# Wider TensorE products in the first stage of a transformer layer kernel: one matmul of 64x128 for four of 64x32

## The chip, the cores and the metric

The kernel runs on one core of one Trainium2 chip. Its time is device microseconds of one execution; the time of a version is the median of several runs. A core has TensorE (in profiles PE for matmuls, PEld for loading the stationary operand), VectorE (DVE), ScalarE (ACT), GpSimd (POOL) and SyncE (SP), which here issues transfers. Matmuls write to PSUM banks; the others read them from there.

## The reference

A parallel transformer layer for 2048 rows of width 512: attention with 32 heads of 16, and an MLP with a hidden width of 1792, both from the same normalised input, summed with the input.

```python
xn = _layernorm(x, axis=-1)
return x + _A_ref(xn, A_wqkv, A_wo) + _B_ref(xn, B_w1, B_b1, B_w2, B_b2)

# _A_ref
qkv = (x @ wqkv).reshape(B, S, 3, H, Dh).transpose(2, 0, 3, 1, 4)
q, k, v = qkv[0], qkv[1], qkv[2]
scores = jnp.einsum("bhqd,bhkd->bhqk", q, k) * (Dh ** -0.5)
o = jnp.einsum("bhqk,bhkd->bhqd", _softmax(scores, axis=-1), v)
return o.transpose(0, 2, 1, 3).reshape(B, S, D) @ wo

# _B_ref
h = _gelu(jnp.einsum("bsd,df->bsf", x, w1) + b1)
return jnp.einsum("bsf,fd->bsd", h, w2) + b2
```

## The kernel before, in words

Numbers are held as two half-precision parts, so that a product of two matrices is three products of parts. Heads are worked on in 8 groups of four; the queries of a group in 4 blocks of 512. A group and a block are one of 32 *blocks* `t`. For each block the scores are computed twice: first as queries by keys, to find each query's maximum (`s_mm`, `s_max`), then as keys by queries (`e_half`), with the maximum already subtracted by extra rows of the operands, followed by the exponential on ScalarE (line 444) and the product with V (`v_half`). A *unit* `u` is a sixteenth of a block: 128 queries by 512 keys for four heads in the first use, 128 keys by 512 queries in the second. The second use runs 19 units (`LEAD`) behind the first.

**Array shape.** Operands of a head lie on 62 or 64 of the 128 rows, two heads above each other. `tiled` (line 200) makes a product of 64 rows from four matmuls of 64 rows by 32 columns, one for each quarter of the output partitions. A product for the upper half of the rows and one for the lower half go to different PSUM banks.

**First stage.** It loads and normalises x, transposes it, projects the first queries, keys and values, sums the absolute values of the weights on ScalarE to find their scales (`total`, line 937; each piece of weights is fetched by a transfer that ScalarE issues, three buffers `wch`), and computes the first 19 units of scores. Its instructions are added to a `Plan` with costs and dependencies; `plan.run` fixes the order on every engine from those costs before the program is built. Within it:
- `twelve` (line 1049) projects with full matmuls of 128x128;
- `side_by_side` runs two groups at once, one on the upper, one on the lower half of the rows, three products of each per step, with `tiled`; there are seven such pairs of groups (`PAIRED`), each of 2 groups x 12 products x 2 halves;
- `score` (line 1114) calls `s_mm` for two heads per step, four heads per unit, and VectorE takes the maximum of each result (line 403).

When the 16 units of block 0 are done, their maxima are reduced (line 369), split into two parts on GpSimd (371 to 373), transposed on TensorE by two small matmuls 32 columns wide (`m_turn`, line 377), copied (line 382), stored to memory (`m_store`, line 358) and read back as rows into the query operand (`m_rows`, line 363). The second use of block 0 needs them.

**Main loop.** From then on `unit` writes out the order by hand: score products, second score products, V products and products of a filler (remaining projections, then the MLP, then the output projection) in turn. All of them but a few at the very end go through 64x32 matmuls, which are recorded at line 174 (`product`), as those of the first stage are. At the very end one group (line 584) has products of 64 rows by 128 columns on one half of the rows.

In the block's query order before, a unit's 128 queries are two runs of 64: columns 64 x qt and 256 + 64 x qt of the block's 512. The layout of the maxima in memory (`m_d`) follows it.

Of the kernel before, what the change touches and what calls it, by code (L numbers as in the profile page):

```python
# [10 lines left out]
F16 = mybir.dt.float16  # L11
# [7 lines left out]
P = 128  # L19
# [8 lines left out]
QB = 512  # L28
NQB = S // QB
NG = H // 4  # L30
# [28 lines left out]
def layer_kernel(ctx: ExitStack, tc: tile.TileContext, x, wqkv, wo, w1, b1, w2, b2, out):  # L59
    nc = tc.nc  # L60
# [3 lines left out]
    def pool(stack, name, bufs=1, space=None, side=None):  # L64
        kw = {k: v for k, v in (("space", space), ("side", side)) if v is not None}
        return stack.enter_context(tc.tile_pool(name=name, bufs=bufs, **kw))
# [4 lines left out]
    dram = pool(ctx, "dram", space=DRAM)  # L71
# [4 lines left out]
    w1_d = dram.tile([NF // 2, P, 2, 2, NC, P], F16, name="w1_d")  # L76
    w2_d = dram.tile([P, 2, NF, D], F16, name="w2_d")
    acc_d = dram.tile([S, D], F32, name="acc_d")
    m_d = dram.tile([NG * NQB, 2, 2, 2, 8, P // 2], F16, name="m_d")
    ot_d = dram.tile([D, 2, S], F16, name="ot_d")  # L80
    den_d = dram.tile([NG * NQB, 2, 4, QB], F32, name="den_d")

# [5 lines left out]
    kst, qst = ([[const.tile([P, 2, QB], F16, name=f"{x}st{i}_{b}") for b in range(NQB)] for i in range(2)] for x in "kq")  # L88
# [83 lines left out]
    def product(user, *args, **kw):  # L172

        p = nc.tensor.matmul(*args, **kw)  # L174
        if user is None:
            return
        if user in goal:
            p._wait_ge(turns[user], counted[user])
            tc.declare_fence(p.ins, group=goal.pop(user))
        newest[user] = p  # L180
# [10 lines left out]
    def enter():  # L191

        for user, ps_ in left.items():
            if ps_:
# [2 lines left out]
                    tc.add_to_no_dep_group(goal[user], p.ins)  # L197
                ps_.clear()

    def tiled(user, dst, lhs, rhs, start, stop):  # L200

        for j in range(0, P, 32):
            product(user, dst[j:j + 32], lhs[:, j:j + 32], rhs, start=start, stop=stop)


    scale_of, wfs = {}, []
# [13 lines left out]
    class Plan:  # L220
# [7 lines left out]
        def add(self, engine, ns, fn, after=(), take=(), free=(), size=0, tail=0, gap=0, small=False, lag=0):  # L228
            t = dict(gap=gap, small=small, lag=lag, e=engine, ns=ns, fn=fn, after=[a for a in after if a], take=take, free=free, size=size, tail=tail,
                     end=None, n=len(self.todo))  # L230
            for key in free:
                self.users.setdefault(key, []).append(t)
            self.todo.append(t)
            return t
# [120 lines left out]
        slot[0] = now  # L355

    def m_store(t, turned):
        nc.sync.dma_start(m_d[t].rearrange("s a j r q -> (s a j r) q"), turned)

    def m_rows(t, a):  # L360
        g, qb = divmod(t, NQB)
        dst = qst[g % 2][qb][64 * a + 62:64 * a + 64].rearrange("j p (s n) -> j p s n", s=2)
        nc.sync.dma_start(dst, m_d[t, :, a].rearrange("s j (p t) q -> j p s (t q)", p=2))

    def m_parts(t):

# [13 lines left out]
    def m_copy(pt):  # L380
        turned = work.tile([64, 64], F16, name="mturned", bufs=2)
        nc.scalar.activation(turned, pt[:64, :64], AF.Copy)
        return turned

    def s_mm(u, n, s):

        t, i = divmod(u, 16)
        g, qb = divmod(t, NQB)
        qt, kb = divmod(i, 4) if t else (i % 4, i // 4)
        ks, qs = kst[g % 2], qst[g % 2]  # L390
        p, a = divmod(n, 2)
        r = slice(64 * a, 64 * a + 62)
        for j in range(0, P, 32):
            c = QB // 2 * (j // 64) + 64 * qt + j % 64
            product(None, s[j:j + 32], qs[qb][r, p, c:c + 32], ks[kb][r, p, :], start=True, stop=True)

    def s_max(u, n, s):

# [7 lines left out]
    def s_half(u, n):  # L406

        s = banks("S")
        s_mm(u, n, s)
        s_max(u, n, s)  # L410

    def s_end(u):

        t, i = divmod(u, 16)
        if i < 15:
            return
        steps, parts = m_parts(t)
        for step in steps:
            step()
        given("dve", 220)  # L420

        def store():

            fresh = cur[0] is not None and 0 < sum(cur[0].at) <= 4
            pt = banks("S" if fresh else "T")
            m_turn(pt, parts)
            m_store(t, m_copy(pt))
            for a in (1, 0):
                m_rows(t, a)

        stores[t] = store

    def e_half(u, n):

        p, a = divmod(n, 2)
        t, kt = divmod(u, 16)
        g, qb = divmod(t, NQB)
        st = banks("T")
        r = slice(64 * a, 64 * a + 64)
        k0 = (kt % 4) * P  # L440
        tiled(None, st, kst[g % 2][kt // 4][r, p, k0:k0 + P], qst[g % 2][qb][r, p, :], True, True)
        pe = work.tile([P, QB], F32, name="pe", bufs=12)
        ptiles[u, n] = pe
        nc.scalar.activation(pe, st, AF.Exp, scale=scale_of[g // 2])  # L444
        given("act", 520)
# [114 lines left out]
    class Group:  # L560
# [15 lines left out]
        def product(self, side):  # L576

            if self.bank is None:
                self.bank, self.key = self.alloc()
            lhs, rhs = self.prods[side % 2][self.at[side % 2]]()  # L580
            start = self.first and self.at == [0, 0]
            if side == 2:
                self.at = [min(self.at[0] + 1, n) for n in self.n]
                nc.tensor.matmul(self.bank, lhs, rhs, start=start, stop=self.last and self.over())
                return
            r = slice(64 * side, 64 * side + 64)
            self.at[side] += 1
            tiled("D", self.bank, lhs[r], rhs[r], start, self.last and self.over())
# [157 lines left out]
    class Halves:  # L746
# [6 lines left out]
        def product(self, side):  # L753
            k = self.at[side]
            if k == self.n[side]:
                return
            if self.banks[side] is None:
                self.keys.append(free_banks["S"].pop(0))
                self.banks[side] = bank_tile(self.keys[-1], "S")
            lhs, rhs = self.prods[side][k]()  # L760
            r = slice(64 * side, 64 * side + 64)
            self.at[side] += 1
            tiled(None, self.banks[side], lhs[r], rhs[r], k == 0, self.at[side] == self.n[side])
            if self.at == self.n:
                self.finish(*[b for b in self.banks if b is not None])
                free_banks["S"] += self.keys
# [84 lines left out]
    with ExitStack() as st1:  # L851
# [262 lines left out]
        def score(u):  # L1114

            t, i = divmod(u, 16)
            qt, kb = divmod(i, 4) if t else (i % 4, i // 4)
            for p in range(2):
                keys = [("S", u, 2 * p + a) for a in range(2)]

                def mm(keys=keys, u=u):
                    s_of[u] = True
                    for key in keys:
                        tl[key] = sb_tile(key)
                        s_mm(key[1], key[2], tl[key])

                old = m_prev[-4:-2]
                s_prev[0] = add("PE", 220, mm, [s_prev[0]] + k_ready[kb] + q_ready[t] + old, take=keys, gap=1230, small=True)
                for key in keys:
                    m_prev.append(add("DVE", 607, lambda key=key: s_max(key[1], key[2], tl[key]), [s_prev[0]], free=[key]))  # L1130
# [11 lines left out]
        for w in (1, 0):  # L1142
# [5 lines left out]
            else:  # L1148
                a = add("POOL", 800, lambda wf=wf, i1=i1: nc.gpsimd.tensor_scalar(tl[wf], tl[wf], i1, 0.0, op0=ALU.mult, op1=ALU.add), [h])
# [5 lines left out]
        a = add("DVE", 90, lambda: nc.vector.tensor_tensor(sexp[:, 0:1], fac0[:, 0:1], fac0[:, 1:2], op=ALU.mult), [chain])  # L1155
        a = add("DVE", 90, lambda: nc.vector.tensor_scalar_mul(sexp[:, 0:1], sexp[:, 0:1], DH ** -0.5), [a])
# [5 lines left out]
        a = add("DVE", 90, lambda: nc.vector.tensor_tensor(amv[:, 2:3], amv[:, 0:1], amv[:, 1:2], op=ALU.max), v_sum)  # L1162
# [54 lines left out]
        a = add("DVE", 220, m_steps[0], m_last)  # L1217
        for step in m_steps[1:]:
            a = add("POOL", 230, step, [a])
# [5 lines left out]
        a = add("PE", 100, turn_m, [a], take=[mkey], small=True)  # L1225
        a = add("ACT", 220, lambda: m_of.append(m_copy(tl[mkey])), [a], free=[mkey])
        put = add("SP", 480, lambda: m_store(0, m_of[0]), [a], size=4)
        for k in (1, 0):
            add("SP", 660, lambda k=k: m_rows(0, k), [put], size=4, tail=E_TAIL)
# [16 lines left out]
        for n, src in enumerate(every[:NM]):  # L1246
            key = ("wch", "m", n)
            dst = am_all[:, 12 + n:13 + n] if n < 2 else am_all[:, n - 2:n - 1] if n < 9 else amx[:, n - 2:n - 1]
# [5 lines left out]
                    nc.tensor.matmul(wp, wo_s[:, 0, 0, 0:P], wo_s[:, 0, 0, :], start=True, stop=True)  # L1254

        nc.vector.memset(wo_s[:, 0, 0, :], 0.0)
        plan.run(fill)
        wfs[1] = [tl["wq", 1, w] for w in range(2)]
        pos[0] = LEAD

# [330 lines left out]
```

## Time and profile before

| | us |
|---|---|
| median of 3 runs | 1458.61 |
| the runs | 1460.75, 1451.14, 1458.61 |
| the profiled execution's own time | 1454.41 |
| its span, first to last instruction | 1452.6 |
| PE busy in the span | 1431.1 (99%) |
| DVE busy | 1348.1 (93%) |
| ACT busy | 1256.6 (87%) |

The profile is of one execution. A row of the timeline has the start, the length, engine, line, operation, what is written and read, the shape (rows*columns of the stationary operand, then the moving operand), a count where several were merged, and in brackets the engine's idle time before it with what ended that. "issue" there means that the engine waited for nothing that the profile shows. PEclk is the share of full clock that TensorE was granted. Matmuls are pipelined: one lasts about 0.38 us from start to end, and the next can start before that.

### The profile page before, as it was taken

The numbers are of one execution on the slowest core, as the hardware profiler recorded it, in microseconds if no ns is written. First come the engines' busy times: TensorE is split into PE (matmuls) and PEld (weight loads), VectorE is DVE, ScalarE is ACT, GpSimd is POOL, SyncE is SP. The second block draws the span as 40 slices with busy tenths as digits, with TensorE's granted clock in tenths as the row PEclk, the third lists the DMA queues.
The fourth block names the chain that finished last, engine by engine and source line by source line (L and its number), as shares of the span: only waits on it lengthen the run. The fifth ranks groups of instructions, "written<-read, shape, count | busy, mean of one in ns | idle before, by whom it ended". The sixth has DMA issues, their size and how long they took to land.

```text
span 1452.6 us, 90738 instructions
## 1 busy us (share of the span) xinstructions
PE 1431.1 (99%) x41221; PEld 973.9 (67%) x41221; DVE 1348.1 (93%) x2236; ACT 1256.6 (87%) x2394; POOL 687.0 (47%) x774
## 2 busy tenths in 40 slices
PE   8889999999999999999999999999999999999998
PEld 4457777776667777666677766666666667666664
DVE  8769999999999999999999999999999999999933
ACT  6558888888999888899988899998889998888885
POOL 5101757664688411368841147783026787212210
PEclk9999999999999999999999999999999999999999
DMA  7550655555223111121122111122102210212313
GB/s 225 167 177 4 202 176 157 183 161 179 83 88 112 50 52 31 47 82 40 49 60 69 28 52 45 43 80 59 37 26 82 56 42 16 59 56 77 119 62 111
DMA packets 111482, 124.98 MB, mean 86 GB/s; under 512 B 21244, under 2 KB 83068, under 8 KB 111096
## 3 DMA queue, kind: packets, MB, share of 16 engines
q1 hardware_dynamic: 103896, 109.74, 24.8%
q10 hardware_dynamic: 7200, 9.44, 2.2%
q8 instruction: 322, 5.28, 1.5%
q14 instruction: 64, 0.52, 0.1%
HBM read 81.66 MB, written 37.34 MB: 82 GB/s over the span
## 4 chain that ended last, share of the span: by engine, by line
PE 92%; DVE 5%; ACT 1%; issue 1%; DMA 0%; SPq 0%; DVEq 0%; POOL 0%; ACTq 0%
PE pD L174 28%; PE pV L174 26%; PE pT L174 21%; PE pS L174 16%; DVE mt L403 4%; DMA wq<-in_A_wqkv_dram 0%; DVE xt L1032 0%; DVE bs L989 0%; ACT xs L1002 0%; PE pT L1049 0%; DVE wvh L1171 0%; ACT xt L1023 0%; ACT pe L444 0%; ACT pe L1002 0%; DVE ac L1466 0%
## 5 line engine op out<-in xcount | busy, mean ns | idle before, releaser
L403 DVE TENSOR_REDUCE mt<-pS 128x1 f32<-128x512 f32 x2029 | 1279.0, 682 | 42.3 <-PE pS L174 14.1
L444 ACT ACTIVATE pe<-pT 128x512 f32<-128x512 f32 x2048 | 1109.1, 599 | 140.1 <-PE pT L174 59.2
L174 PE MATMUL pV<-pe,vv 64*32 64x512 f32 x8192 | 1087.3, 591 | 0.3
L174 PE MATMUL pT<-qst,kst 64*32 64x512 f16 x8192 | 705.4, 378 | 0.6 <-ACT pe L444 0.3
L174 PE MATMUL pS<-kst,qst 62*32 62x512 f16 x8116 | 628.1, 378 | 1.3 <-issue 0.8
L174 PEld LDWEIGHTS <-qst 62*32 62x32 f16 x8192 | 312.4, 91 | 187.6 <-issue 37.9
L174 PE MATMUL pD<-xb,wc 64*32 64x512 f16 x5376 | 363.3, 376 | 0.0
L174 PE MATMUL pD<-w_s,g 64*32 64x512 f16 x5376 | 361.1, 376 | 0.0
L174 PEld LDWEIGHTS <-kst 64*32 64x32 f16 x8192 | 281.2, 91 | 97.0 <-issue 25.0
L174 PEld LDWEIGHTS pV<-pe,vv 64*32 64x32 f32 x8192 | 241.4, 106 | 12.6 <-PE pV L174 5.6
L174 PEld LDWEIGHTS <-wc 64*32 64x32 f16 x5376 | 160.7, 92 | 44.8 <-issue 0.3
L174 PEld LDWEIGHTS <-g 64*32 64x32 f16 x5376 | 162.9, 92 | 38.7
L174 PE MATMUL pD<-xt,wqk_h 64*32 64x512 f16 x2400 | 159.4, 376 | 0.0
L371 POOL TENSOR_SCALAR mparts<-mx 128x16 f16<-128x16 f32 x32 | 6.5, 203 | 296.5 <-DVE mx L369 286.3
L1433 POOL TENSOR_TENSOR xa<-xa,yt 128x512 f32<-128x512 f32 x16 | 20.5, 1280 | 166.2 <-ACT yt L1431 166.1
L174 PEld LDWEIGHTS <-wqk_h 64*32 64x32 f16 x2592 | 78.2, 93 | 20.9 <-issue 1.2
L1387 POOL TENSOR_TENSOR t<-t,hh 128x512 f32<-128x512 f32 x56 | 71.8, 1282 | 4.7
L1380 POOL TENSOR_TENSOR t<-t,hh 128x512 f32<-128x512 f32 x56 | 71.7, 1281 | 4.5
L1385 POOL TENSOR_TENSOR t<-hh 128x512 f32<-128x512 f32 x56 | 58.2, 1040 | 21.6 <-ACT hh L1408 19.2
L1382 POOL TENSOR_TENSOR g<-t,g 128x512 f16<-128x512 f32 x56 | 65.2, 1164 | 4.7
L501 POOL TENSOR_TENSOR osb<-osb,rb 128x512 f32<-128x512 f32 x31 | 39.8, 1284 | 48.1 <-ACT pe L444 29.5
L174 PE MATMUL pD<-wo_s,oc 64*32 64x512 f16 x816 | 54.7, 376 | 0.0
(161 smaller groups left out, 965.8 us busy)
## 6 DMA issues: line engine op xcount, KB each, us to landing
wc<-w_d SPq DMA_DIRECT2D x56, 256.0 KB
qk_d<-stg SPq DMA_DIRECT2D x32, 256.0 KB
rb<-den_d SPq DMA_DIRECT2D x124, 64.0 KB
wch<-in_B_w_dram ACTq DMA_DIRECT2D x14, 512.0 KB
wch<-in_B_w_dram SPq DMA_DIRECT2D x28, 256.0 KB
w_d<-wsp SPq DMA_DIRECT2D x28, 256.0 KB
kst<-qk_d SPq DMA_DIRECT2D x64, 96.0 KB
qst<-qk_d SPq DMA_DIRECT2D x64, 96.0 KB
```

The lines of the kernel that those rows point to most:

```text
L174: p = nc.tensor.matmul(*args, **kw)
L371: lambda: nc.gpsimd.tensor_scalar(parts[:, :, 0], mx[:, 0], 1.0 / MROW, 0.0, op0=ALU.mult, op1=ALU.add),
L403: nc.vector.reduce_max(mt_of[t][:, n // 2 + n % 2 * 2, qt, kb:kb + 1], s, axis=AX.X)
L444: nc.scalar.activation(pe, st, AF.Exp, scale=scale_of[g // 2])
L501: pooled((1280, lambda: nc.gpsimd.tensor_tensor(osb, osb, rb, op=ALU.mult)), (620, lambda: nc.gpsimd.tensor_scalar(ot[:, 0], osb, 1.0, 0.0 ...
L1380: (1280, lambda: nc.gpsimd.tensor_tensor(t1, t1, hh, op=ALU.mult)),
L1382: (1160, lambda: nc.gpsimd.tensor_tensor(g[:, 1, f, :], t1, g[:, 0, f, :], op=ALU.subtract)),
L1385: pooled((1040, lambda: nc.gpsimd.tensor_tensor(t1, hh, hh, op=ALU.mult)), (620, lambda: nc.gpsimd.tensor_scalar(t1, t1, 1.0, 1.0 / GELU_A ...
L1387: (1280, lambda: nc.gpsimd.tensor_tensor(t1, t1, hh, op=ALU.mult)),
L1433: add = lambda: nc.gpsimd.tensor_tensor(xa, xa, yt, op=ALU.add)
```

## The change

In the first stage a product of 64 (or 62) rows is one matmul of 128 columns. After `plan.run` the width goes back to 32 for all that follows. So that the same code serves for scores with either width, a unit's 128 queries are now adjacent columns of the block, in the first stage and in the main loop, and the layout of the maxima in memory follows: it is now scattered when it is stored and read back in one run per row.

```diff
-    m_d = dram.tile([NG * NQB, 2, 2, 2, 8, P // 2], F16, name="m_d")
+    m_d = dram.tile([NG * NQB, 2, 2, 2, 4, 2, P // 2], F16, name="m_d")
...
+    wide = [32]
+
     def tiled(user, dst, lhs, rhs, start, stop):
 
-        for j in range(0, P, 32):
-            product(user, dst[j:j + 32], lhs[:, j:j + 32], rhs, start=start, stop=stop)
+        for j in range(0, P, wide[0]):
+            product(user, dst[j:j + wide[0]], lhs[:, j:j + wide[0]], rhs, start=start, stop=stop)
...
     def m_store(t, turned):
-        nc.sync.dma_start(m_d[t].rearrange("s a j r q -> (s a j r) q"), turned)
+        nc.sync.dma_start(m_d[t].rearrange("a j p t s q -> (s a j p t) q"), turned)
 
     def m_rows(t, a):
         g, qb = divmod(t, NQB)
-        dst = qst[g % 2][qb][64 * a + 62:64 * a + 64].rearrange("j p (s n) -> j p s n", s=2)
-        nc.sync.dma_start(dst, m_d[t, :, a].rearrange("s j (p t) q -> j p s (t q)", p=2))
+        nc.sync.dma_start(qst[g % 2][qb][64 * a + 62:64 * a + 64], m_d[t, a].rearrange("j p t s q -> j p (t s q)"))
...
         r = slice(64 * a, 64 * a + 62)
-        for j in range(0, P, 32):
-            c = QB // 2 * (j // 64) + 64 * qt + j % 64
-            product(None, s[j:j + 32], qs[qb][r, p, c:c + 32], ks[kb][r, p, :], start=True, stop=True)
+        tiled(None, s, qs[qb][r, p, P * qt:P * qt + P], ks[kb][r, p, :], True, True)
...
         nc.vector.memset(wo_s[:, 0, 0, :], 0.0)
+        wide[0] = P
         plan.run(fill)
+        wide[0] = 32
         wfs[1] = [tl["wq", 1, w] for w in range(2)]
```

More of the change, by code (lines that the diff above doesn't have):

```diff
@@ L357, in m_store @@
     def m_store(t, turned):
-        nc.sync.dma_start(m_d[t].rearrange("s a j r q -> (s a j r) q"), turned)
+        nc.sync.dma_start(m_d[t].rearrange("a j p t s q -> s (a j p t) q"), turned)
     def m_rows(t, a):
         g, qb = divmod(t, NQB)
-        dst = qst[g % 2][qb][64 * a + 62:64 * a + 64].rearrange("j p (s n) -> j p s n", s=2)
-        nc.sync.dma_start(dst, m_d[t, :, a].rearrange("s j (p t) q -> j p s (t q)", p=2))
+        nc.sync.dma_start(qst[g % 2][qb][64 * a + 62:64 * a + 64], m_d[t, a].rearrange("j p t s q -> j p (t s q)"))
     def m_parts(t):
```

## The prediction

> **What bounds the kernel now.** I read the page first: total, instruction stream, chain.
>
> ```profile
> span 1452.6 us, 90738 instructions
> PE 1431.1 (99%) x41221; PEld 973.9 (67%) x41221; DVE 1348.1 (93%) x2236; ACT 1256.6 (87%) x2394; POOL 687.0 (47%) x774
> q8 instruction: 322, 5.28, 1.5%
> PE 92%; DVE 5%; ACT 1%; issue 1%; DMA 0%; SPq 0%; DVEq 0%; POOL 0%; ACTq 0%
> ```
>
> TensorE is the bound nearly everywhere: 99% busy, 92% of the chain that ended last. The third line is kept for later: the instruction queue moved 5.28 MB in 322 packets, 16.4 KB each. TensorE's 41221 matmuls and 41221 weight loads, 82442 instructions, make that 64 bytes an instruction, so one packet is 256 TensorE instructions.
>
> Then the table of busy time by stretch: the main loop, and the second half of the first stage (from 54 us to TensorE's first main-loop product at 102.4).
>
> ```profile
> 400.00:1400.00 1000.00, 998.82 (x29536) 689.22 (x29528) 970.02 (x1580) 899.78 (x1720) 485.50 (x550) 1.00 0.20 58
> 54.00:102.40 48.40, 40.52 (x1326) 24.26 (x1303) 33.16 (x55) 21.04 (x40) 2.90 (x5) 0.93 0.64 196
> ```
>
> Columns: stretch, its length, busy us with counts of PE, PEld, DVE, ACT, POOL, then granted TensorE clock, DMA share, GB/s. The main loop leaves TensorE 1.2 us idle in 1000: what the first stage gains or loses, the loop hands on to the end. The stage's second half is different: TensorE idles 48.40 - 40.52 = 7.88 us, and its clock is 0.93. The waits by engine in 0 to 100 us, and TensorE's timeline, say where:
>
> ```profile
> PE pT L174 <- issue: 4.5, 3, 2.3
> PE pV L174 <- issue: 3.4, 1, 3.4
> ```
>
> ```profile
> 61.58 0.39 PE L174 MATMUL pT<-wvh,xt 64*32 64x512 f16 x2 [1.71 <-issue]
> 67.50 0.39 PE L174 MATMUL pT<-wvh,xt 64*32 64x512 f16 x2 [2.26 <-issue]
> 77.13 0.39 PE L174 MATMUL pT<-wvh,xt 64*32 64x512 f16 x2 [0.56 <-issue]
> 87.88 0.39 PE L174 MATMUL pV<-kst,qst 62*32 62x512 f16 x2 [3.35 <-issue]
> ```
>
> All of it is four stalls (1.71 + 2.26 + 0.56 + 3.35 = 7.88) in which TensorE waits for no tile, no semaphore, no transfer of data. What lies between and after them:
>
> ```profile
> 54.00:59.80 5.80, 5.80 (x222) 3.07 (x199) 5.80 (x11) 1.21 (x3) 0.00 (x0) 1.00 0.93 286
> 61.60:65.20 3.60, 3.60 (x128) 2.06 (x128) 2.55 (x5) 1.15 (x2) 0.00 (x0) 1.00 0.90 236
> 68.20:71.70 3.50, 3.50 (x80) 1.80 (x72) 1.65 (x3) 2.03 (x5) 0.02 (x1) 0.51 0.07 9
> 77.20:84.50 7.30, 7.30 (x256) 4.50 (x256) 6.56 (x11) 2.43 (x5) 0.07 (x1) 1.00 0.63 165
> 88.70:92.20 3.50, 3.50 (x86) 1.93 (x71) 1.04 (x3) 2.12 (x4) 0.58 (x3) 0.51 0.53 167
> ```
>
> Between the first and second stall TensorE ran 128 + 128 = 256 instructions, one packet of the instruction queue; between the third and fourth 256 + 256, two packets. So I read "issue" as: **TensorE ran out of instructions**, because the next packet came late behind data (DMA share 0.93 and 0.90 ahead of the first two stalls). The main loop runs 29.5 matmuls per us, about the stage's pace, at DMA share 0.20, and hardly stalls so. After the two longest stalls comes a second price: 3.5 us each at clock 0.51, so 2 x 3.5 x 0.49 = 3.4 us of work lost.
>
> **The change part by part.**
>
> (1) *Count.* The stage has 7 pairs of groups x 2 x 12 products x 2 halves = 336 half-row products, and 19 x 4 = 76 score products: 412 products, formerly 4 matmuls each, now 1. Removed: 412 x 3 = 1236 matmuls and as many weight loads, 2472 instructions, 2472 / 256 = 9.7 packets.
>
> (2) *Array time.* Two half-row products, one per half, form a pair of eight matmuls now.
>
> ```profile
> 52.76 0.38 PE L174 MATMUL pD<-wvh,xt 64*32 64x512 f16 x4
> 52.77 0.38 PE L174 MATMUL pT<-wvh,xt 64*32 64x512 f16 x4
> 52.98 0.38 PE L174 MATMUL pD<-wvh,xt 64*32 64x512 f16 x4
> 1446.23 1.84 PEld L584 LDWEIGHTS <-ot 64*128 64x128 f16 x10 [0.66 <-DVE ot L540]
> 1446.23 2.33 PE L584 MATMUL pD<-wo_l,ot 64*128 64x512 f16 x10 [0.17 <-DVE ot L540]
> ```
>
> A pair takes 52.98 - 52.76 = 0.22 us, its halves 0.01 apart. The last two rows are the nearest to the new form: ten products of 64x128 on one half, (2.33 - 0.38) / 9 = 0.217 us apart, so a wide weight load hides behind the matmul before it, on its own half too. No row shows two wide products on both halves at once. Bounds: 0.217 us a pair (side by side) to 0.43 (one after the other). I take 0.217: the halves do run together at width 32, two writers per output partition included. Gain in array time: nothing.
>
> (3) *Stalls.* In 54 to 102.4 us 1326 matmuls become 332, with the loads 663 instructions over some 37 us, 18 per us against 54; a packet lasts 14 us, not 4.7. The latest was 3.35 us late. I take all four stalls and both slow-clock stretches as gone: -7.88 - 3.4 = **-11.3 us**. Bounds: 0 (packets late by more) to -11.3.
>
> (4) *Mode.* A change of array shape shows here:
>
> ```profile
> 29.79 0.60 PE L1049 MATMUL pT<-xt,wqk_h 128*128 128x512 f16 x2
> 30.32 0.41 PE L174 MATMUL pS<-kst,qst 62*32 62x512 f16 x8
> 30.66 0.82 PE L1049 MATMUL pT<-xt,wqk_h 128*128 128x512 f16 x3
> ```
>
> From the second 128x128 product (29.79 + 0.22 = 30.01) to the scores 0.31 us, and 0.34 back, against 0.22: about 0.1 us a switch. Their number stays where scores stand among 128x128 work. New ones: line 377, still 32 wide, now stands alone among wide products (2), and the main loop's start (1): +0.3 us. If the switch between 128x128 and 64x128 is cheaper, up to 2 us come back (some 20 switches, mostly under other waits). The Trainium skill, "TensorEngine Tiling (Array Packing)", Key Properties, says that changing the tiling mode drains TensorE; it speaks against this edit. Taken in full, each of the three would wait out a matmul's tail, 0.38 - 0.22 = 0.16 us, +0.5 us in all; the rows' 0.1 us is less, and the rows stand.
>
> (5) *What is late next.* Without stalls TensorE has 40.52 - 3.4 = 37.1 us of work in that stretch. VectorE:
>
> ```profile
> L403 DVE TENSOR_REDUCE mt<-pS 128x1 f32<-128x512 f32 x39 | 25.1, 683 | 10.3 <-PE pS L174 10.2
> L403 DVE TENSOR_REDUCE mt<-pV 128x1 f32<-128x512 f32 x14 | 9.5, 682 | 4.9 <-PE pV L174 4.9
> ```
>
> 33.16 us busy, and its 15 us of idleness are waits for TensorE: less than 37.1, it follows. DMA: 0.64 x 48.4 = 31 us of full use, at the best share of the rows above (0.93) 33.3 us: it fits too, but barely. ScalarE sums weight pieces in order, and each sum waits for its piece:
>
> ```profile
> 78.92 0.37 ACTq L929 DMA_DIRECT2D wch<-in_B_w_dram  x1
> 84.19 1.06 ACT L937 ACTIVATE wch<-wch 128x1024 f32<-128x1024 f32 x1 [3.39 <-DMA wch<-in_B_w_dram]
> 89.06 0.60 ACT L1187 ACTIVATE vv<-pT 128x512 f32<-128x512 f32 x1 [3.72 <-PE pT L174]
> 104.61 4.37 ACT L444 ACTIVATE pe<-pT 128x512 f32<-128x512 f32 x8
> ```
>
> A piece takes 84.19 - 78.92 = 5.3 us here. Up to 89 us ScalarE has 3.72 us of slack left after that wait; later sums wait likewise, and behind the last of them stand the main loop's first exponentials (104.61, 2.2 us behind TensorE's product). The path of the row maxima is as tight:
>
> ```profile
> 93.96 0.53 SPq L358 DMA_DIRECT2D m_d<-mturned  x1
> 97.38 1.83 SPq L363 DMA_DIRECT2D qst<-m_d  x2
> 102.37 0.40 PE L174 MATMUL pT<-qst,kst 64*32 64x512 f16 x4
> ```
>
> From the store to the second issue's end 5.25 us, and if landing takes what the store's did (3.4 us at most), 102.6: about when TensorE arrives. This chain moves with TensorE, since line 377 starts it. I charge **+2.5 us** for both: nothing if the pieces keep pace, 11 if transfers keep today's times, nearest to the low end since every waiting row here but the pieces' names TensorE.
>
> (6) *New layout of the maxima.* Same bytes, same issues on SP's queue (one store, two reads per block), longer runs in the read. TensorE's waits from 103 to 1440 us, all of them:
>
> ```profile
> PE pS L377 <- DVE mt L403: 1.0, 5, 0.2
> PE pS L174 <- issue: 0.8, 1, 0.8
> PE pD L174 <- issue: 0.3, 1, 0.3
> PE pT L174 <- ACT pe L444: 0.3, 1, 0.3
> ```
>
> None is for a transfer: three units of TensorE work hide the read. Cost nothing; uncovered, it would be some 0.1 us x 31 blocks. Main-loop scores read other columns, same shapes: nothing.
>
> Sum: -11.3 + 0.3 + 2.5 = -8.5; 1454.41 - 8.5 = **1446 us**. The median shown, 1458.61, lies 4.2 above the profiled execution, and the three runs spread over 9.6 us; I guess that stalls differ between runs, which no view shows. Against the median 1446 is -0.9%.
>
> **The rivals.**
>
> *Given back (0.22).* Stalls go, but the pieces or the maxima set the stage's end. For: DMA at 31 of 37 us, ScalarE's 3.39 us wait. Against: the slack of 3.72. Half or more comes back: 1449 to 1454, say 1451.
>
> *Stalls stay (0.10).* If a packet is late however slowly it is used up, because nothing asks for it earlier, fewer packets still mean fewer stalls: of four perhaps one or two remain: 1450 to 1455.
>
> *The halves don't share (0.06), slower.* If two wide products exclude each other, each pair costs 0.217 us more: 1326 / 8 = 166 pairs in the stretch, +36, less 11.3: 1479; with all 206 pairs of the stage 1488. It decides from 0.217 + 11.3 / 166 = 0.285 us a pair; *sharing in part* (0.04), about there, leaves the time at 1454. For: no row shows such a pair. Against: the halves 0.01 us apart above. The Trainium skill, "TensorE: Matmul & The Clock Gate", Part 3, gives 3.07x for four row tiles; read as a rate, a pair would take 0.22 x 4 / 3.07 = 0.28 us and cancel the gain. The trace disagrees at width 32: eight tiles per 0.22 us.
>
> **How the numbers follow.** Forecast 0.58 (1442 to 1449), given back 0.22, stalls stay 0.10, no sharing 0.06, sharing in part 0.04. Range: the low end takes every stall and the cheaper switches, 1454.4 - 11.3 - 2 = 1441; the high end the two middle rivals and the spread between runs, 1457; outside are no sharing and a tail. About 1% is what a measurement of this kernel can tell from no change; that is 1444.0 below the median. Two fifths of the forecast lie under it (0.23), and a little of the rivals; no sharing and a tail lie over 1473: faster 0.25, same 0.67, slower 0.08.
>
> **What would show it.** Right: 1236 fewer of both PE counts, some 10 fewer packets; no wait for "issue" over 1 us before 95 us, clock 1.00 from 54 us on; pairs still 0.22 us apart; line 444's first row near 95 us. Wrong: pairs over 0.28 us; DVE or ACT waiting on DMA where TensorE waited for "issue"; stalls that move into the main loop's start, where 59 instructions per us begin while pieces still land.

## The result and the profile after

| | before | changed |
|---|---|---|
| median of 20 runs, us | 1458.22 | 1449.67 |
| lowest to highest | 1451.14 to 1462.15 | 1446.51 to 1453.42 |
| the profiled execution's own time | 1454.41 | 1448.31 |

The ratio of the changed kernel to the one before is 0.9942, interval 0.9931 to 0.9953: 8.55 us less by the medians. The line numbers behind the edit shift by one (the exponential is line 443, the sums are line 936).

From the page of the changed kernel: total, engines, the instruction queue.

```profile
span 1446.5 us, 88266 instructions
PE 1430.4 (99%) x39985; PEld 963.1 (67%) x39985; DVE 1348.1 (93%) x2236; ACT 1257.0 (87%) x2394; POOL 687.2 (48%) x774
q8 instruction: 312, 5.11, 1.5%
```

1236 matmuls and 1236 loads are gone, and 10 packets of instructions. The first stage from 54 us to TensorE's first main-loop product, and 3.4 us that follow a little later (columns as before: length, busy time of each engine with counts, clock, DMA share, GB/s):

```profile
54.00:89.90 35.90, 35.90 (x332) 17.86 (x328) 32.67 (x55) 21.14 (x40) 2.90 (x5) 1.00 0.80 248
...
94.50:97.90 3.40, 3.40 (x60) 1.45 (x53) 1.16 (x2) 2.15 (x5) 0.00 (x0) 0.50 0.00 0
```

In the first row TensorE has no idle time at all, at clock 1.00; the four stalls on "issue" are gone. The pairs, in TensorE's timeline, run as they did:

```profile
52.69 0.38 PE L174 MATMUL pD<-wvh,xt 64*128 64x512 f16 x1
52.69 0.38 PE L174 MATMUL pT<-wvh,xt 64*128 64x512 f16 x1
52.91 0.37 PE L174 MATMUL pD<-wvh,xt 64*128 64x512 f16 x1
```

Both halves start at 52.69, the next pair at 52.91: 0.22 us a pair, side by side at full width. The main loop's start then has something that it had not:

```profile
89.91 0.40 PE L174 MATMUL pT<-qst,kst 64*32 64x512 f16 x4
...
94.16 0.40 PE L174 MATMUL pT<-qst,kst 64*32 64x512 f16 x4 [1.80 <-ACT pe L443]
```

```profile
85.71 1.06 ACT L936 ACTIVATE wch<-wch 128x1024 f32<-128x1024 f32 x1 [1.95 <-DMA wch<-in_B_w_dram]
...
92.47 1.06 ACT L936 ACTIVATE wch<-wch 128x1024 f32<-128x1024 f32 x1 [1.38 <-DMA wch<-in_A_wo_dram]
93.44 0.19 ACT L936 ACTIVATION_READ_ACCUMULATOR wch<-wch 128x1 f32 x1
93.53 2.04 ACT L443 ACTIVATE pe<-pT 128x512 f32<-128x512 f32 x4
```

TensorE arrives 12.46 us earlier (89.91 against 102.37), but ScalarE's first exponential comes only at 93.53, behind the sum of the last weight piece, and that sum waited 1.38 us for its transfer. TensorE stands for 1.80 us, and right behind that its clock is at 0.50 for 3.4 us, 1.7 us of work. A later row of ScalarE's timeline, the same four exponentials of each kernel, gives what is left:

```profile
123.90 2.10 ACT L444 ACTIVATE pe<-pT 128x512 f32<-128x512 f32 x4
```

```profile
114.33 2.10 ACT L443 ACTIVATE pe<-pT 128x512 f32<-128x512 f32 x4
```

9.57 us ahead: 2.9 of the 12.46 were given back at the start of the loop (the 1.80 and the 1.7, less 0.45 us for which TensorE stood here, from 102.4 to 110 us, in the kernel before). The spans differ by 6.1: the loop of this execution took another 3.5 us longer than that of the profiled one before. That is looked into at the end of the experiments.

### The profile page after: what moved, and what is told of

Same layout as the page of the kernel before. It is cut to its first block, busy times and chain, and to the rows that moved or that the text cites. A ratio compares the mean times of both kernels' runs of the same rounds, so it can differ in the third digit from the quotient of the medians.

```text
span 1446.5 us, 88266 instructions
## 1 busy us (share of the span) xinstructions
PE 1430.4 (99%) x39985; PEld 963.1 (67%) x39985; DVE 1348.1 (93%) x2236; ACT 1257.0 (87%) x2394; POOL 687.2 (48%) x774
## 4 chain that ended last, share of the span: by engine, by line
PE 90%; DVE 4%; DMA 2%; issue 2%; ACT 1%; POOL 0%; SPq 0%; DVEq 0%; ACTq 0%; POOLq 0%
PE pD L174 27%; PE pV L174 26%; PE pT L174 19%; PE pS L174 16%; DVE mt L402 3%; DMA qk_d<-stg 1%; DMA pe<-in_A_x_dram 0%; DMA wch<-in_A_wo_dram 0%; DMA qst<-qk_d 0%; DMA wq<-in_A_wqkv_dram 0%; DVE bs L988 0%; PE pD L1048 0%; ACT xt L1022 0%; DVE wvh L1170 0%; DVE xt L1031 0%
## 5 line engine op out<-in xcount | busy, mean ns | idle before, releaser
L174 PE MATMUL pS<-kst,qst 62*32 62x512 f16 (+1 forms) x7945 | 626.7, 378 | 0.9 <-DVE mt L402 0.9
L174 PEld LDWEIGHTS <-qst 62*32 62x32 f16 (+1 forms) x7964 | 308.2, 91 | 186.2 <-issue 33.5
L174 PEld LDWEIGHTS <-wqk_h 64*32 64x32 f16 (+1 forms) x2448 | 75.8, 92 | 22.3 <-issue 1.3
```

## Experiments

My theory: TensorE ran out of instructions, because their packets came late behind the stage's data, and fewer instructions let a packet last until the next is there. Rivals: the layout and the quicker read of the maxima bring the gain; or each instruction has its price (8.5 us over 2472). What is given back hangs on ScalarE's chain of pieces.

### Only the layout

```diff
-        wide[0] = P
         plan.run(fill)
```

> The new query order and layout of the maxima, but the width stays 32 in the first stage (no instruction goes). If the gain comes from TensorE no longer running out of instructions: the same time as before, ratio 0.999 to 1.001, about 8 us of 'issue' stalls between 54 and 95 us and a slow clock behind the long ones. If the layout or the read of the maxima brings the gain: 0.994 to 0.997.

Measured 0.9992 (0.9977 to 1.0007), 1455.74 us. TensorE's waits from 54 to 100 us:

```profile
PE pT L174 <- issue: 3.1, 3, 1.7
PE pV L174 <- issue: 3.1, 1, 3.1
```

The new order of the queries and the new layout change nothing that can be measured; the stalls are there, 6.2 us of them, and behind the longest the clock is at 0.50 from 86.4 to 89.7 us. The first rival falls.

### Two matmuls of 64 columns

```diff
-        wide[0] = P
+        wide[0] = 64
```

> First stage in matmuls of 64x64: two a product, 824 matmuls and 824 loads fewer than with 32, against 1236 with 128. Running out of instructions is a threshold: some 36 instructions per us in the stage, a packet of 256 lasts 7 us, the latest came 3.4 us after a packet of 4.7 us was used up (8.1), so at most one stall under 1.5 us remains and nearly the whole gain comes: ratio 0.994 to 0.996. If the gain is a price per instruction (8.5 us over 2472): two thirds, 0.996 to 0.997, with stalls still there.

Measured 0.9947 (0.9929 to 0.9965), 1448.65 us. The stage until TensorE's first product of the loop, and TensorE's waits:

```profile
54.00:91.10 37.10, 37.10 (x682) 24.91 (x674) 33.68 (x57) 21.17 (x41) 2.90 (x5) 1.00 0.78 237
```

```profile
PE pT L174 <- ACT pe L443: 1.6, 1, 1.6
PE pT L174 <- ACT vv L1186: 0.8, 1, 0.8
```

With two thirds of the instructions removed there is no stall on "issue" left, and the gain can't be told from the whole. A price per instruction (0.996 to 0.997) isn't excluded by this interval alone; that all four stalls vanish at 36 instructions per us is what a threshold gives. The half pieces, further down, decide on that rival.

### One part of the change alone

Products of the pairs wide, scores narrow:

```diff
-        tiled(None, s, qs[qb][r, p, P * qt:P * qt + P], ks[kb][r, p, :], True, True)
+        for j in range(0, P, 32):
+            c = P * qt + j
+            product(None, s[j:j + 32], qs[qb][r, p, c:c + 32], ks[kb][r, p, :], start=True, stop=True)
```

> Only the pairs of groups go 128 wide, the scores between them stay 32 wide (2016 instructions fewer). No stall on 'issue' by the first theory; but each score among the pairs now changes the array's shape twice, some 27 scores x 2 x 0.1 us = 5 us on TensorE between 54 and 95 us: ratio 0.996 to 0.999. If a switch between 64x128 and 64x32 costs nothing: 0.994 to 0.995.

Measured 0.9962 (0.9947 to 0.9977), 1450.09 us. Its timeline of TensorE around one score, and its first product of the loop:

```profile
56.05 0.81 PE L174 MATMUL pT<-xt,wqk_h 64*128 64x512 f16 x6
56.79 0.40 PE L174 MATMUL pS<-kst,qst 62*32 62x512 f16 x4
...
57.13 0.82 PE L174 MATMUL pT<-xt,wqk_h 64*128 64x512 f16 x6
...
96.65 0.40 PE L174 MATMUL pT<-qst,kst 64*32 64x512 f16 x4
```

The score and the way back take 57.13 - 56.79 = 0.34 us where a pair takes 0.22, and three pairs and the way into the score 0.74 instead of 0.65: 0.1 us a switch, between two column widths as between row modes. No stall on "issue" came, TensorE entered the loop 6.7 us later than in the changed kernel (96.65 against 89.91; 5.4 were worked out from 27 scores), and yet by the ratios (0.9962 against 0.9942, intervals overlapping, measured at different times) it is only some 3 us slower. Part of the late entry cost nothing, since what the changed kernel loses there (1.80 us and the slow clock) didn't occur: 0.3 us of waiting was left, at clock 1.00.

Scores wide, pairs narrow (`tiled` always with 32; the first stage's scores, in `s_mm`, in one matmul, an edit not shown here):

```diff
-        for j in range(0, P, wide[0]):
-            product(user, dst[j:j + wide[0]], lhs[:, j:j + wide[0]], rhs, start=start, stop=stop)
+        for j in range(0, P, 32):
+            product(user, dst[j:j + 32], lhs[:, j:j + 32], rhs, start=start, stop=stop)
```

> Only the scores go 128 wide, the pairs of groups stay 32 wide (456 instructions fewer, 18% of the change). Stalls on 'issue' remain, a little shorter (5 to 8 us), and the same 5 us of switches come on top: ratio 1.000 to 1.004. If a switch costs nothing and the gain is a price per instruction: 0.999.

Measured 0.9985 (0.9972 to 0.9998), 1453.21 us: a miss. The waits of TensorE from 54 to 100 us in its profile:

```profile
PE pT L174 <- issue: 0.7, 2, 0.4
```

Only 0.7 us of stalls, not 5 to 8. The switches slow TensorE (2429 instructions in 46 us, 53 per us against 54), and 456 instructions are gone; neither seems enough for so much. Its runs lie between 1451.43 and 1458.04 us, so other executions may stall more; that isn't shown. How much slack a packet needs stays open.

### The data in front of the packets

The kernel before and the changed one, with the 18 weight pieces fetched and summed by half:

```diff
-                tl[key] = raw(key, "wch", [P, 4 * W], 3).rearrange("p (a b) -> p a b", b=src.shape[2])
+                tl[key] = raw(key, "wch", [P, 4 * W], 3).rearrange("p (a b) -> p a b", b=src.shape[2])[:, :src.shape[1]]
...
-            low(total(1150, key, dst, piece_in(key, src, q_ready[0], queue="ACT", tail=30000), done=[key]))
+            low(total(1150, key, dst, piece_in(key, src[:, :src.shape[1] // 2], q_ready[0], queue="ACT", tail=30000), done=[key]))
```

> The kernel before, with every instruction of TensorE kept, but the 18 weight pieces that ScalarE sums in the first stage are fetched and summed by half (the scales come from half of each piece): 4.7 MB less data to transfer in the stage. If packets of instructions come late because they stand behind that data: 'issue' stalls between 54 and 95 us fall from about 8 us to under 2, no slow clock behind them, ratio 0.992 to 0.996. If TensorE runs out because it uses instructions up too fast whatever the data: stalls stay, ratio 0.998 to 1.000.

Measured 0.9957 (0.9944 to 0.9971), 1448.84 us, with every one of TensorE's instructions kept. Its stage and its waits:

```profile
54.00:94.00 40.00, 37.53 (x1315) 21.69 (x1303) 32.90 (x55) 15.23 (x39) 2.91 (x5) 1.00 0.51 151
```

```profile
PE pV L174 <- issue: 1.2, 1, 1.2
PE pT L174 <- issue: 1.1, 2, 1.0
```

The DMA share falls from 0.64 to 0.51, the stalls from 7.88 to 2.3 us (I had put under 2), and the clock stays at 1.00. TensorE enters the loop at 94.0 with the same work in front of it (1315 matmuls from 54 us on, against 1326). So it was not the number of instructions by itself, and the rival of a price per instruction falls: no instruction went, and most of the gain came. ScalarE's sums get shorter here too (15.23 us busy instead of 21.04), but in the profile before TensorE waits for ScalarE nowhere in this stretch.

The traces also keep a record of every packet of the instruction queue, and with these the theory can be read off directly. In the kernel before, times in us:

| TensorE stops | packet's transfer starts | packet has landed | TensorE goes on | landing to going on |
|---|---|---|---|---|
| 59.87 | 59.30 | 60.25 | 61.58 | 1.3 |
| 65.24 | 64.59 | 65.99 | 67.50 | 1.5 |
| 76.57 | 74.12 | 76.12 | 77.13 | 1.0 |
| 84.53 | 85.64 | 86.67 | 87.88 | 1.2 |

The profiles of the kernel before, of the layout alone, of the half pieces and of the wide scores have 13 stalls on "issue" between 54 and 95 us. Each of them ends 1.0 to 1.5 us after a packet has landed, and within a profile they always lie 256, 512 or 768 matmuls and weight loads apart: 256, 512 and 512 in the kernel before. That data are in front is plainest in the fourth row: the packet's transfer starts only 1.1 us after TensorE has stopped, where the DMA share falls from 0.87 (84.6 to 85.6 us) to 0.16 (85.7 to 87.9). In the third the packet takes 2.00 us, where most take 0.9 to 1.1. What decides when a packet is asked for, no trace here shows.

> The changed kernel with the same halved pieces. If what is given back at the main loop's start is ScalarE's wait for the last pieces: TensorE's 1.8 us wait for line 443 and the slow clock behind it are gone, 2 to 4 us below the changed kernel, ratio to before 0.991 to 0.993. If something else sets the stage's end there: 0.994 as the changed kernel.

Measured 0.9923 (0.9909 to 0.9936), 1444.71 us, 3.4 us below the changed kernel measured beside it (1448.11). Its profile shows no wait of TensorE at all from 54 to 100 us, and clock 1.00 in 95 to 102.4. What is given back hangs on the pieces.

### A version that gives less back

The last two pieces (of `wo`) are fetched as four of half the size into buffers that held rows of x, early in the stage:

```diff
-        for n, src in enumerate(every[:NM]):
+        for n, src in enumerate(every[:NM - 2]):
...
+        def wo_in(key, n):
+            def fn():
+                tl[key] = raw(key, "pe", [P, QB], 12).rearrange("p (a b) -> p a b", b=D)
+                nc.scalar.dma_start(tl[key], wov[:, n:n + 1, :])
+            return add("ACT", 420, fn, q_ready[0], take=[key], size=256, tail=30000)
+
+        for n in range(4):
+            key = ("xp", "wo", n)
+            low(total(600, key, amx[:, 14 + n:15 + n], wo_in(key, n), done=[key]))
...
```

> The changed kernel, with the last two weight pieces fetched as four smaller ones into buffers that the rows of x have left, early in the stage, so that the chain of three buffers is two pieces shorter. If the chain of pieces is what TensorE waits for at the main loop's start: no wait there, 2 to 4 us below the changed kernel (ratio 0.991 to 0.993). If the early pieces crowd the first projections instead: 0.995 to 0.998.

> The changed kernel once more beside these, as their reference: ratio 0.993 to 0.996. A second profile of it also tells whether the 1.8 us wait at the main loop's start and the slow clock behind it come again; both are expected.

Measured 0.9938 (0.9924 to 0.9951), 1446.04 us, against 0.9945 (0.9932 to 0.9959), 1448.11 us, for the changed kernel: 2.1 us less, intervals overlapping, and a ratio between the two that were expected (0.991 to 0.993, 0.995 to 0.998). The second profile of the changed kernel, an execution of 1453.23 us, is the clearest picture of the loop's start, in TensorE's waits from 54 to 100 us and the stretch of low clock behind them:

```profile
PE pT L174 <- ACT pe L443: 1.7, 1, 1.7
PE pT L174 <- ACT vv L1186: 0.9, 1, 0.9
PE pT L174 <- DMA qst<-m_d: 0.9, 1, 0.9
```

```profile
97.30:104.10 6.80, 6.72 (x92) 2.71 (x91) 2.58 (x4) 3.66 (x8) 0.00 (x0) 0.50 0.01 2
```

Here the maxima's rows (`qst<-m_d`) are late too, and the clock is at 0.50 for 6.8 us, which costs 3.4 us of work.

Once more, side by side:

> The version with the last two weight pieces moved, once more beside the changed kernel, since their intervals overlapped: if the wait at the main loop's start is what it saves, 2 us below the changed kernel (1 to 4); if the first comparison was chance, the same within 0.5 us.

> The changed kernel as the reference beside it: ratio to before 0.994 to 0.995; its profile with a wait of 1 to 2 us for line 443 at the main loop's start.

Measured 0.992 (0.9902 to 0.9938), 1444.40 us, against 0.9955 (0.994 to 0.9971), 1448.69 us. Now the intervals are apart: 4.3 us, a little over what was expected. The changed kernel's third profile has the wait for line 443 again, 1.8 us, and a clock of 0.77 in 95 to 102.4. In both profiles of the version with the moved pieces TensorE waits for nothing from 54 to 100 us. This version beats both kernels.

It has a price that this stretch doesn't show. TensorE's waits from 30 to 54 us in its first and in its second profile have each a row that is much longer than in the changed kernel:

```profile
PE pS L174 <- DMA kst<-qk_d: 2.5, 1, 2.5
```

```profile
PE pS L174 <- DMA kst<-qk_d: 3.4, 1, 3.4
```

At this place the changed kernel waits 0.9 us for VectorE or 0.5 us for the keys at most. So the early pieces seem to crowd the keys that are read back there, much as the second half of the expectation had it; that isn't shown beyond these two rows. TensorE enters the loop at 91.31 and 94.09 us, later than in the first profile of the changed kernel (89.91), and the version wins all the same. What it would gain without that wait wasn't measured.

### The main loop from run to run

From the start of one and the same exponential, the 31st of block 0, to the end of the span, counted in each trace:

| profile | that start, us | from there to the end, us |
|---|---|---|
| before | 124.88 | 1327.8 |
| only the layout (same loop, same width) | 123.70 | 1331.8 |
| before, half pieces | 116.10 | 1330.3 |
| products wide | 119.04 | 1328.6 |
| scores wide | 122.54 | 1328.1 |
| width 64 | 117.10 | 1330.8 |
| changed, three profiles | 115.31, 120.09, 115.95 | 1331.2, 1331.4, 1331.8 |
| changed, half pieces | 112.49 | 1334.0 |
| `wo` pieces moved, two profiles | 113.13, 115.91 | 1329.2, 1329.9 |

The profiled execution before had the shortest loop of the twelve, 0.3 to 6.3 us under the others, 3.0 in the middle. The layout alone, whose stage is the same as before, had 4 more; its interval, up to 1.0007, leaves no room for 4 us as a cost of the layout. Some of it is the same cause as in the stage. TensorE's waits from 105 to 1440 us in the profile with the layout alone:

```profile
PE pD L174 <- issue: 2.5, 3, 1.4
PE pS L378 <- DVE mt L402: 1.0, 5, 0.2
PE pS L174 <- issue: 0.6, 1, 0.6
```

3.1 us on "issue", where the profile before had 1.1 from 103 us on and the changed kernel 1.4. The longest loop of all (changed, half pieces) has 3.1 too. The rest of the difference between loops isn't broken down.

## Why the prediction was right, point by point

- **What bounds** and the meaning of "issue": held. Removing instructions (width 64, 128) removes the stalls, less data (half pieces) cuts them from 7.88 to 2.3 us, changing the layout leaves them. Every one of these stalls ends shortly after a packet of instructions has landed.
- **(1) Count**: 1236 and 1236, 10 packets, as worked out.
- **(2) Array time** nothing: 0.22 us a pair, both halves at once. The rival that the halves don't share falls, in full and in part. With it falls the reading of the Trainium skill, "TensorE: Matmul & The Clock Gate", Part 3, by which a pair would have taken 0.28 us (0.29 with the 0.22 that the prediction wrote, 0.28 with 0.217).
- **(3) Stalls and slow clock** -11.3: all gone within the stage. The size is that of one execution: the profile of the layout alone has 6.2 us of stalls and one slow stretch of 3.4 us, some 7.9 instead of 11.3. With the +0.3 of (4) the entry into the loop should have come 11.0 us earlier; it came 12.46 earlier. Of the 1.4 more, one place shows 0.21, a score and the next pair behind it, where two groups change halves. TensorE's timeline before and after:

```profile
74.18 0.59 PE L174 MATMUL pS<-kst,qst 62*32 62x512 f16 x8
74.61 0.40 PE L174 MATMUL pD<-wvh,xt 64*32 64x512 f16 x4
```

```profile
68.28 0.38 PE L174 MATMUL pS<-kst,qst 62*128 62x512 f16 x2
68.50 0.38 PE L174 MATMUL pD<-wvh,xt 64*128 64x512 f16 x1
```

0.43 us from the one to the other became 0.22. The rest isn't broken down.

- **(4) Mode**: 0.1 us a switch, confirmed by the version with narrow scores. The three new switches (+0.3) weren't measured by themselves.
- **(5) What is late next** +2.5: the chain named, ScalarE's pieces in front of the first exponentials, is the one that TensorE meets, and 2.9 us were given back in the profiled execution (the 1.80 of waiting and the 1.7 of slow clock, less what TensorE had stood there before). The first exponentials, put near 95 us, came at 93.53. Clock 1.00 from 54 us on, named as a sign of being right, didn't hold behind 94.5 us, and a wait at the loop's start, named as a sign of being wrong, did come: for ScalarE, though, not on "issue". The execution of 1453.23 us came to the same exponential 4.8 us later (120.09 against 115.31 in the table). So how much is given back differs from one execution to the next, and the median may contain some of both. By the time alone, 1449.67 lies among the times of the rival "given back" (1449 to 1454) and just outside the forecast's own (1442 to 1449). In the profile a quarter came back, not half or more, so the mechanism is the forecast's, and the time is off by the base.
- **(6) Layout** nothing: 0.9992.
- **The base**: the sum, -8.5 us, meets the medians' -8.55, and that it does so within 0.1 us is luck. In the profiles the stage gained 9.57 at the 31st exponential where the sum had 8.5, the spans differ by 6.1, and the two later comparisons of the same two kernels gave 7.0 us (1455.12 to 1448.11) and 7.3 (1455.95 to 1448.69). The time, 1446, is 3.7 us too low, because it starts from the profiled execution, 3.8 us below the median of 20 runs (1454.41 against 1458.22). I had put that difference down to stalls in the stage that vary, which would vanish with the change. By the table it lay rather in the main loop, where the change leaves TensorE's instructions as they were: there that execution was the shortest of all, and its stage was no shorter than that of the layout alone. No execution at the median of the kernel before was profiled, so this is likely and not shown. What failed is the step from a profiled execution to a median, and with it "the loop hands on to the end" as a statement about single executions; a saving taken off the median itself (1458.6 - 8.5 = 1450.1) would have been within 0.5 us of the time.

## What to carry to other kernels

Idle time of TensorE that waits for nothing, in distances of whole packets of instructions, was here an instruction stream that came late: look at the DMA share ahead of each stall and at when the packet lands, and make either the instructions or the data in front of them fewer. A stage that gets shorter meets the transfers that it used to cover: the next gain here was in moving the last of them forward, not in TensorE. And take a saving off the median of the runs, not off the one execution that was profiled.

## What was not expected

- The main loop, which has the same instructions on TensorE in all these kernels (the two with the old layout read the queries in another order), took 1327.8 to 1334.0 us in twelve profiles, at DMA share 0.20 in most of it.
- When TensorE enters the loop before ScalarE can follow, an earlier entry is worth about half: 6.7 us between the first profiles of products wide and of the changed kernel, of which 3.7 are left at the 31st exponential, and some 3 us in the ratios.
- Behind the waits of 1.80 us (changed kernel, first profile) and 1.71 us (second) at the loop's start TensorE's clock was at 0.50 for 3.4 and 6.8 us, which costs 1.7 and 3.4 us, as much as the wait or more. It isn't the length of the wait alone: behind the stall of 1.71 us in the kernel before the clock stayed at 1.00.
